# Two more head pairs take VectorE's transposition of P, and a new order table

## The chip, the cores and the metric

The kernel runs on one core of a Trainium2 chip. The metric is device time in microseconds (us), from the first to the last instruction of one execution with what lies around it; lower is better. Five engines work side by side and wait for each other through semaphores: TensorE (PE in the rows, its weight loads PEld), VectorE (DVE), ScalarE (ACT), GpSimd (POOL) and SyncE (SP), which issues every transfer of this kernel.

## The reference

Causal attention over 4 batches of 12 heads, 448 tokens, head size 64, and then a gated MLP over the 768 joined features. Cut to what matters:

```python
scores = q @ k.T / sqrt(64), masked to the lower triangle
P = exp(scores - rowmax);  x = (P / rowsum(P)) @ v        # per batch and head
h = gelu(x @ w_in);  u, v = h[..., :512], h[..., 512:]
v_s = w_sg @ layernorm(v) * g_ln + b_sg                   # over the 448 tokens
out = x + (u * v_s) @ w_out
```

## The kernel before

Heads are taken two at a time: 24 pairs, 0 to 23, six to a batch. The steps of a pair are these. A load brings q and k (`qk`), another brings v (`vraw`). TensorE computes the scores in two groups into PSUM (L639, 8 matmul records a group). VectorE adds the mask and takes the row maximum (L653). ScalarE takes the exponential into P and sums its rows (L661). The sums are inverted, transposed and spread over the partitions through DRAM (`rd`, `rb`). P must then be transposed, since TensorE contracts over the partitions, and the transposed P, called `B`, is multiplied with v (L738, "PV"). VectorE scales the result (`xt`, L766), and it is stored (`xd`) and split into a high and a low part for the MLP.

The transposition of P has two forms, chosen by `flip = p >= FLIP`. With `FLIP = 8`, pairs 0 to 7 use TensorE: four groups of four 128x128 transpositions into PSUM (`tx`, `ty`, L708), each group moved to `B` by ScalarE (L715) or, for one group of each pair of batch 0, by VectorE (L713). Pairs 8 to 23 use VectorE, which transposes blocks of 32x32 (L696, two instructions a pair) into the array `A`, and four transfers of 256 KB, issued by SP (L700), carry it from `A` to `B`:

```python
for z in range(2):
    dve(PW, lambda z=z: nc.vector.transpose(A[ia]..., P[ib[z]]), Pk[z] + [kp], Ak, Tt, 1.105)
for i in (0, 2, 1, 3):
    dma(lambda i=i: nc.sync.dma_start(out=B_.t[:, 512 * i:512 * i + 512],
                                      in_=PP[ia][32 * i:32 * i + 32]...), Ak, [(B_, i)], Te, ...)
```

There is one `A` (`NA = 1`): it is the third of the three double P buffers, which pairs 2 and 5 also use as plain P. So a pair's transposition on VectorE waits until the transfers of the pair before have read `A`, and pair 6's would wait for TensorE's transpositions of pair 5. `B` has two buffers. PV takes the same 1,024 columns for each of the two heads in either form, in 20 matmul records a pair with the first form and in 32 with the second.

Between the pairs of a batch TensorE works on the MLP of the batch before, in groups of up to three matmuls (L796): v, u, s and o. The weights are loaded in parts, split by ScalarE, VectorE and GpSimd; w_out comes in 16 parts (`wout`, L564 to L574) while pairs 6 to 8 are under way.

The order of the work is written out in the table `ORDER`, which lists every step by its number (1,927 steps; 551 of them TensorE's, 245 SP's), in the order of planned starts. Each engine issues its own steps in that order, so an instruction that waits holds up everything behind it on its engine, and a transfer that waits on SP holds up every later transfer. Eight PSUM banks are shared by all of it.

Of the kernel before, what the change touches and what calls it, by code (L numbers as in the profile page):

```python
# [50 lines left out]
FLIP = 8  # L51
# [367 lines left out]
def attention_gated_mlp(ctx: ExitStack, tc: tile.TileContext, qk, vP, w_in, g_ln, w_sgT, b_sg, w_out, out):  # L419
# [200 lines left out]
    def pair(p):  # L620
# [3 lines left out]
        per = STEP[b]  # L624
        flip = p >= FLIP
        kp, ks = "P" if p % (NP // 2) else "P0", "sm" if p % NS else "sm0"
# [379 lines left out]
```

## Time and profile before

| | us |
|---|---|
| median of 3 runs | 354.4 (353.96 to 354.82) |
| the profiled execution, its own time | 355.62 |
| its span, first to last instruction | 353.8 |
| what lies around the span | 1.8 |
| TensorE busy / VectorE / ScalarE / GpSimd | 339.1 / 260.0 / 196.6 / 149.9 |

A busy time is the union of an engine's instructions in the span; the rest of the span it was idle. Busy is not the same as needed: a matmul whose end is late counts as busy too.

### The profile page before, as it was taken

How to read it: one execution, taken by the hardware profiler on the slowest of the kernel's cores; microseconds unless marked ns; L12 is line 12 of the kernel's file. 1: busy time of each engine (PE TensorE's matmuls, PEld its weight loads, DVE VectorE, ACT ScalarE, POOL GpSimd, SP SyncE). 2: the span in 40 equal slices, each digit the busy share in tenths (PEclk: the TensorE clock that was granted, in tenths of full speed). 3: DMA queues.
4: the chain of work that ended last, by engine and by line, in shares of the span. 5: the costliest groups of instructions: out<-in, count | busy, mean ns of one | idle time of the engine just before them, and what ended most of it. 6: DMA issues, size and time to landing. Idle time of an engine off the chain costs nothing.

```text
span 353.8 us, 6879 instructions
## 1 busy us (share of the span) xinstructions
PE 339.1 (96%) x2231; PEld 269.2 (76%) x2231; DVE 260.0 (73%) x762; ACT 196.6 (56%) x658; POOL 149.9 (42%) x200
## 2 busy tenths in 40 slices
PE   7698999989999999999999999998999999999995
PEld 3455667657888778776898888776898898889995
DVE  2999978689999988756899987377897721258613
ACT  2999987777856957237443885218344700135410
POOL 4567887236977720010653641001265700242550
PEclk9999999999999999999999999999999999999999
DMA  7988987697855887797575786889465455400004
GB/s 237 374 284 292 304 287 228 196 287 210 248 123 173 219 238 250 242 298 248 151 173 128 235 236 176 269 240 295 121 200 126 139 119 196 155 2 1 0 2 156
DMA packets 37972, 69.50 MB, mean 196 GB/s; under 512 B 3888, under 2 KB 18992, under 8 KB 37936
## 3 DMA queue, kind: packets, MB, share of 16 engines
q1 hardware_dynamic: 37936, 69.06, 64.2%
q8 instruction: 18, 0.29, 0.3%
q14 instruction: 18, 0.15, 0.1%
HBM read 39.68 MB, written 12.58 MB: 148 GB/s over the span
## 4 chain that ended last, share of the span: by engine, by line
PE 69%; DMA 13%; DVE 9%; ACT 4%; SPq 3%; issue 1%; POOL 1%; DVEq 0%; POOLq 0%
PE m L796 47%; PE o L738 10%; PE s L639 8%; DMA B<-P 5%; ACT P L661 3%; DVE s L653 3%; DVE P L696 2%; DMA vn<-in_w_in_dram 2%; DMA out_dram<-res 2%; DMA rb<-rd 2%; PE tx L708 1%; DMA g<-in_w_out_dram 1%; DMA res<-xd 1%; PE ty L708 1%; SPq L680 1%
## 5 line engine op out<-in xcount | busy, mean ns | idle before, releaser
L661 ACT ACTIVATE P<-s,ngm 64x64 f32<-64x64 f32 (+3 forms) x240 | 100.3, 432 | 38.6 <-DVE ngm L653 18.4
L653 DVE CUSTOM_DVE_ANT_0 s<-s,mask 128x192 f32<-128x192 f32 (+3 forms) x192 | 75.3, 444 | 5.8 <-PE s L639 5.8
L796 PE MATMUL m<-win,x 128*128 128x512 f32 (+1 forms) x264 | 67.1, 399 | 0.0
L796 PE MATMUL m<-x,win 128*128 128x448 f32 x288 | 64.1, 370 | 1.8 <-ACT P L661 1.1
L796 PE MATMUL m<-g,wout 128*128 128x448 f32 x288 | 62.1, 368 | 0.0
L796 PEld LDWEIGHTS m<-x,win 128*128 128x128 f32 x288 | 53.3, 188 | 8.4 <-ACT P L661 1.9
L796 PEld LDWEIGHTS m<-g,wout 128*128 128x128 f32 x288 | 53.4, 188 | 5.4 <-issue 0.2
L796 PEld LDWEIGHTS m<-win,x 128*128 128x128 f32 (+1 forms) x264 | 46.8, 183 | 12.5 <-ACT P L661 0.6
L639 PE MATMUL s<-qk 64*128 64x448 f32 (+3 forms) x384 | 53.5, 403 | 1.8 <-DMA qk<-in_qk_dram 1.7
L639 PEld LDWEIGHTS s<-qk 64*128 64x128 f32 (+1 forms) x384 | 33.6, 178 | 23.2 <-issue 13.2
L661 ACT ACTIVATION_READ_ACCUMULATOR P<-s,ngm 128x1 f32 (+1 forms) x240 | 49.6, 207 | 0.0
L738 PE MATMUL o<-B,vraw 128*64 128x64 f32 (+4 forms) x672 | 47.2, 292 | 2.0 <-ACT P L661 1.4
L777 POOL TENSOR_TENSOR x<-xt,x 128x448 fp32r<-128x448 f32 x24 | 27.8, 1162 | 46.1 <-ACT x L776 45.9
L696 DVE STREAM_TRANSPOSE P<-P 128x1024 f32<-128x1024 f32 x32 | 39.3, 1233 | 9.5 <-DMA B<-P 4.4
L738 PEld LDWEIGHTS o<-B,vraw 128*64 128x64 f32 x672 | 33.0, 137 | 15.9 <-issue 6.3
L796 PE MATMUL m<-wsg,vn 128*128 128x448 f32 x176 | 39.6, 369 | 0.0
L851 POOL TENSOR_TENSOR mv<-mv,mhalf 128x1 f32<-128x1 f32 (+1 forms) x16 | 9.4, 592 | 67.7 <-DVE mv L849 67.2
L796 PEld LDWEIGHTS m<-wsg,vn 128*128 128x128 f32 x176 | 32.7, 188 | 3.2 <-issue 0.2
L804 ACT ACTIVATE tmp<-m 128x448 f32<-128x448 f32 (+1 forms) x28 | 15.2, 565 | 22.7 <-PE m L796 21.1
L807 ACT ACTIVATE tmp<-tmp 128x448 f32<-128x448 f32 (+2 forms) x32 | 18.9, 603 | 14.4 <-DVE tmp L805 14.1
L653 DVE DVE_READ_ACCUMULATOR2_ANT ngm<- 128x1 f32 (+1 forms) x192 | 25.7, 134 | 0.0
L805 DVE SCALAR_TENSOR_TENSOR tmp<-tmp,m 128x448 f32<-128x448 f32 (+1 forms) x28 | 17.3, 633 | 11.2 <-ACT tmp L804 11.1
(77 smaller groups left out, 379.5 us busy)
## 6 DMA issues: line engine op xcount, KB each, us to landing
B<-P SPq DMA_DIRECT2D x64, 256.0 KB
qk<-in_qk_dram SPq DMA_DIRECT2D x24, 448.0 KB
vn<-in_w_in_dram SPq DMA_DIRECT2D x12, 512.0 KB
vraw<-in_vP_dram SPq DMA_DIRECT2D x24, 256.0 KB
rb<-rd SPq DMA_DIRECT2D x24, 256.0 KB
xd<-xt SPq DMA_DIRECT2D x24, 224.0 KB
res<-xd SPq DMA_DIRECT2D x9, 448.0 KB
out_dram<-res SPq DMA_DIRECT2D x9, 448.0 KB
```

The source lines that it names most:

```text
L639: nc.tensor.matmul(out=s[z][bk].t[0:w, col:col + n], lhsT=qk_.t.rearrange("p a s -> p (a s)")[r, q0:q0 + w], rhs=qk_.t[r, 1, 0:n], start=T ...
L653: nc.vector.tensor_tensor_reduce(out=o, in0=o, in1=mk, scale=-0.125, scalar=3e38, op0=ALU.add, op1=ALU.min, accum_out=ngm[ib[z]][c][0:m])
L661: act(n, lambda c=c, m=m, k0=k0, n=n, bk=bk, col=col, off=off, kc=kc, i=i, z=z: nc.scalar.activation(out=P[i][0:m, off:off + n], in_=s[z][ ...
L696: dve(PW, lambda z=z: nc.vector.transpose(A[ia][:, :, :, z, :].rearrange("p g t k -> p t g k"), P[ib[z]]), Pk[z] + [kp], Ak, Tt, 1.105)
L708: nc.tensor.transpose(out, P[ib[z]][:, col:col + 128], ident)
L738: nc.tensor.matmul(out=dst(o.t[r]), lhsT=vr.t[:, c, r], rhs=src(z), start=first and n == 0, stop=last and n == len(lst) - 1)
L777: pool_tt(S, lambda: nc.gpsimd.tensor_tensor(out=y.t[:, S + 64:], in0=x.t, in1=f(y.t)[:, 0:S], op=ALU.subtract), [x, y], [(y, 1)], Ty)
L796: nc.tensor.matmul(out=ps.t[0:l().shape[1], 0:n], lhsT=l(), rhs=rr(), start=(k == 0), stop=(k == len(mms) - 1))
L804: act(n, lambda: nc.scalar.activation(out=z(), in_=h(), func=AF.Square), [ps], [t], at)
L805: dve(n, lambda: nc.vector.scalar_tensor_tensor(out=z(), in0=z(), scalar=1.0 / GC, in1=h(), op0=ALU.add, op1=ALU.mult), [ps], [t], at)
L807: act(n, lambda: nc.scalar.activation(out=z(), in_=z(), func=AF.Tanh, scale=GS * GC), [], [t], at, True)
L851: od.add("pool", 0.46, lambda mv=mv, m=m: nc.gpsimd.tensor_tensor(out=mv.t[0:m, 1:2], in0=mv.t[0:m, 1:2], in1=mhalf[0:m], op=ALU.pow), ["s ...
```

## The change

`FLIP` goes from 8 to 6: pairs 6 and 7, the first two of batch 1, take the second form of the transposition, and their v is laid out for it on the host. `ORDER` is replaced as a whole; it now has 1,923 steps (543 of TensorE, 409 instead of 417 of ScalarE, 542 instead of 538 of VectorE, 253 instead of 245 of SP). No other line differs. The diff, with the table cut:

```diff
-FLIP = 8
+FLIP = 6
...
 ORDER = (
-    1, 2, 84, 12, 4, 3, 118, 18, 5, 128, 6, 0, 172, 7, 24, 8, 162, 9, 10, 348, 85, 13, 14, 86, 15, 87, 16, 89, 11,
...
-    1921, 1897, 1922, 1898, 1902, 1925, 1923, 1890, 1926, 1924, 1903, 1891, 1904, 1892, 1905,
...
+    1921, 1919, 1910, 1922, 1920, 1911, 1912, 1886, 1913, 1897, 1887, 1914, 1891, 1888, 1892, 1904, 1893, 1905,
+    1894, 1898, 1906, 1899, 1907, 1900, 1901,
 )
```

Read by steps, SP's part of the table around pairs 6 and 7 was `p5 rb, p4 xd, p10 qk, p6 rd, p7 v, p6 rb, p5 xd, p7 rd, wout x4, p11 qk, wout x4, p7 rb, wout x3, p8 v, p6 xd, wout x2, p8 B x3`. It becomes `p5 rb, p4 xd, p10 qk, p6 B x4, p6 rd, p5 xd, p7 v, wout x5, p7 rd, p6 rb, wout x3, p11 qk, p7 rb, wout x2, p7 B x4, wout x2, p12 qk, wout x3, p6 xd, p8 v, p8 rd, p8 B x3`.

## Rows read from the trace of the kernel before

**Rows 1.** The page: busy time and share by engine; granted TensorE clock in 40 slices.
```profile
PE 339.1 (96%) x2231; PEld 269.2 (76%) x2231; DVE 260.0 (73%) x762; ACT 196.6 (56%) x658; POOL 149.9 (42%) x200
...
PEclk9999999999999999999999999999999999999999
```

**Rows 2.** Stretches: us, busy of PE, PEld, DVE, ACT, POOL; clock, DMA share, GB/s.
```profile
0.00:10.00 10.00, 6.40 (x23) 2.76 (x23) 3.80 (x20) 3.13 (x5) 5.45 (x28) 1.00 0.79 257
10.00:40.00 30.00, 25.74 (x188) 15.96 (x190) 29.18 (x105) 29.46 (x114) 20.97 (x22) 1.00 0.92 316
...
50.00:80.00 30.00, 28.61 (x212) 19.95 (x212) 22.24 (x82) 22.96 (x85) 14.20 (x22) 1.00 0.75 239
...
80.00:120.00 40.00, 40.00 (x276) 32.82 (x275) 39.77 (x122) 29.06 (x91) 30.38 (x45) 1.00 0.68 190
160.00:250.00 90.00, 88.06 (x586) 71.73 (x584) 71.13 (x190) 49.69 (x176) 25.66 (x29) 1.00 0.73 208
...
350.00:354.00 4.00, 0.29 (x2) 0.00 (x0) 0.96 (x2) 0.00 (x0) 0.00 (x0) 0.79 0.43 152
```

**Rows 3.** Groups of instructions: TensorE's and VectorE's transpositions, ScalarE's moves, the multiplication with v.
```profile
L708 PE MATMUL ty<-ident,P 128*128 128x128 f32 x64 | 10.4, 279 | 0.7 <-ACT B L715 0.4 <-ACT P L661 0.2
...
L715 ACT ACTIVATE B<-tx 128x512 f32<-128x512 f32 x16 | 9.7, 609 | 1.5 <-PE tx L708 1.4
...
L696 DVE STREAM_TRANSPOSE P<-P 128x1024 f32<-128x1024 f32 x32 | 39.3, 1233 | 9.5 <-DMA B<-P 4.4 <-ACT P L661 3.2 <-DMA vraw<-in_vP_dram 1.9
```

**Rows 4.** The chain that ended last, TensorE's pieces: start us, us, what.
```profile
37.53 1.89 PE o L738 x20
...
45.01 1.06 PE s L639 x8
46.08 0.59 PE tx L708 x4
46.66 0.44 PE ty L708 x4
...
102.98 0.61 PE m L796 x3
...
113.70 2.85 PE s L639 x24
116.56 4.68 PE m L796 x22
...
123.17 1.92 PE o L738 x32
```

**Rows 5.** The same chain where it leaves TensorE.
```profile
71.02 5.10 DMA g<-in_w_out_dram
76.14 0.38 ACT g L566
76.52 1.15 ACT P L661 x6
77.72 1.96 PE o L738 x20
...
156.16 7.00 DMA B<-P
163.29 1.25 DVE P L696
...
231.83 4.74 DMA B<-P
```

**Rows 6.** The page's transfers: queue with packets, MB, share of 16 engines; issues.
```profile
q1 hardware_dynamic: 37936, 69.06, 64.2%
...
B<-P SPq DMA_DIRECT2D x64, 256.0 KB
```

**Rows 7.** SP's timeline from 55 to 85 us: start, us, issues.
```profile
68.41 3.04 SPq L564 DMA_DIRECT2D g<-in_w_out_dram  x4
...
83.36 2.58 SPq L700 DMA_DIRECT2D B<-P  x3
```

188 rows, old and new, of the table ORDER are left out of this document.

## Prediction

> **What bounds the kernel now.** I read the busy times first, then the stretches, then the chain of work that ended last, and then the transfers. TensorE is busy for 339.1 of 353.8 us and its granted clock is full in every slice [rows 1], so what is left to gain is either TensorE work or TensorE's 14.7 us of idle time. The stretches say where that idle time lies: 7.9 us in the first 40 us (10 less 6.40, 30 less 25.74), 1.4 us between 50 and 80, 1.9 us between 160 and 250, 3.5 us after the last matmul; nothing elsewhere [rows 2]. In the first part VectorE and ScalarE are full (29.2 and 29.5 of 30 us), so there TensorE follows them. From 80 to 120 VectorE is full again, 39.8 of 40, but TensorE is too [rows 2]. The chain runs along TensorE and leaves it in two ways that matter here: a late w_out part holds ScalarE, which then holds pair 6's PV, and late transfers into B hold VectorE's next transposition [rows 5].
>
> **What the change removes.** Pairs 6 and 7 each lose four groups of four transpositions. A record lasts 279 ns [rows 3], but they overlap: a group that follows work of the same tile shape ends 0.44 us after it [rows 4]. Eight groups by 0.44 are 3.5 us off TensorE, which has no idle time around them but the 1.4 us above. ScalarE loses eight moves of 0.609 us [rows 3], 4.9 us; worth nothing by itself, since at 50 to 80 ScalarE has 7 us idle already [rows 2].
>
> By the Trainium skill ("VectorE: DVE Perf Modes", "The three transpose paths") a 128x128 transposition takes TensorE 390 ns (bf16); 32 of them would be 12.5 us, and the time some 343. The row decides for 0.11 us each, as the groups' ends are 0.44 us apart.
>
> **What it adds on TensorE.** PV of a pair goes from 20 records in 1.89 us to 32 in 1.92 [rows 4]: 0.06 us for both. The new table costs more: counted along TensorE's steps, the tile shape (scores, PV, all others) changes 87 times instead of 81. A change costs 0.15 us before a transposition (0.59 against 0.44), 0.17 before scores (1.06 for one group; 2.85 for three, so 0.9 for each further one) and 0.2 before MLP matmuls (22 in 4.68 us, where 3 without a change take 0.61) [rows 4]. Six more are 0.9 to 1.3 us; I take 1.2, near the upper price, since the changes into MLP groups are among the six. TensorE's work falls by 3.5 - 0.06 - 1.2 = 2.2 us.
>
> **What it adds elsewhere.** VectorE gets four transpositions of 1.233 us [rows 3], 4.9 us. The table puts pair 6's just before pair 8's scores and pair 7's around pair 9's; by the TensorE work in front of them that is about 60 to 78 us in the old trace. Between 50 and 80 VectorE has 7.8 us idle [rows 2], so I cost them at nothing there; without that cover they cost up to 4.9 us. Eight transfers of 256 KB are 2.1 MB; at 64.2% of 353.8 us for 69.06 MB [rows 6] they take 6.9 us of all 16 engines, where 25% of 30 us, 7.5 us, are free [rows 2]. On SP they take 0.86 us each (three in 2.58) [rows 7], 6.9 us too. Behind pair 6's four on SP stand its sums (`rd`), pair 5's store, pair 7's v, and the first w_out parts; behind pair 7's four stand w_out parts, pair 12's q and k, and pair 8's v. Who waits for those is ScalarE and VectorE, which split w_out in order with the exponentials and row maxima behind. Pair 6's PV stands about 16 us of TensorE work behind its last transfer in the table, pair 7's about 17; a landing takes 4.7 to 7.0 us from its issue [rows 5]. So the transfers themselves hide.
>
> **The idle time under the new table.** Four parts.
> The first 40 us: the table moves steps, but takes no work from VectorE or ScalarE there, and the same steps come up to pair 5's scores. I take no change, bounds -1 to +1.
> The 1.4 us before pair 6's PV: ScalarE stood 5.1 us behind a w_out part [rows 5]. In the new table, each w_out part has 3.9 us or more of TensorE work between issue and first use instead of 3.3, and pair 6's PV comes after more of u. I take half of the stall away, 0.7; bounds -1.4 to +1.4 (as long a stall again).
> 160 to 250 us: with one A, the next pair's transposition waits for the last transfer of the pair before. Between these two the old table puts at least 5.9 us of TensorE work; the new one puts 4.8, 4.9, 5.1 and 5.2 in four places (pairs 12, 21, 18 and 11), and is otherwise alike (median 6.9 against 6.8): late landings may have been in the search's objective, but these margins did not grow. Were every landing at the slow end, 7.0, the sum of what is short would be 5.3 us in the old table and 10.0 in the new. VectorE did wait 4.4 us for B in the old trace [rows 3], and TensorE's idle time there was 1.9, 0.44 of that. So the new table's 4.7 us more would be 2.1 us of TensorE; at the fast end, 4.7, nothing. I take 0.7, bounds -1.9 (all of that idle time goes) to +2.1.
> The end: the last groups and the last store are the same steps, no change.
> The parts cancel: -0.7 and +0.7.
>
> **Sum.** The profiled execution's 355.62 us becomes 353.4; its span 351.6. It stands 1.2 us above the median of the runs, 354.4, so for the median the forecast is 354.4 - 2.2 = **352.2 us**.
>
> **The rivals.** (1) The gain is eaten by late landings: the four short places and the later w_out parts cost TensorE 1.5 to 2.9 us more than now. For it: those margins lie at the fast end of what landings took. Against it: TensorE has MLP work in hand there (88.1 of 90 us busy [rows 2]). Time 353.7 to 355.1.
> (2) VectorE becomes the bound from pair 6 on, and the kernel gets slower. The place is the stretch up to 120 us: if pair 7's two transpositions (5 us of TensorE work apart in the table) slip past 80, they fall where VectorE has 0.2 us free in 40 [rows 2], and every later row maximum and GELU step of batch 1 slips with them. The price is up to 4.9 us; from 2.9 us on it outweighs the gain and shows as slower. Time 355.2 to 357.1. For it: idle time of 7.8 us for 4.9 us of work leaves only 2.9, and steps in order can't use all of it. Against it: pair 8's transpositions move back by some 10 us of TensorE work to make room, and pair 8 was early before (its PV stood 17 us behind its transfers).
> The Trainium skill's rule on the same page ("Rules for kernel authors") is to give a full 128x128 transposition to TensorE where PSUM will do, which is what this change leaves; it points to this rival.
> (3) The table is worth more than the transpositions: the stalls at pair 6 and at 160 to 250 both go, and a little of the start: -1.4, -1.9 and -0.5 on top of 2.2. Time 348.4 to 350.
>
> **How the numbers follow.** Forecast, 350 to 353.7 us: 0.58. Rival 1, 353.7 to 355.1: 0.17. Rival 2: 0.13. Rival 3: 0.12. Faster by over 0.2% (0.7 us, about what a measurement of this kernel can tell from no change) are the forecast and rival 3: 0.70; within: 0.17; slower: 0.13. The range leaves out the better half of rival 3 and the worse part of rival 2: 349.3 to 355.6. The likeliest case's own range is 350.6 to 353.7.
>
> **What would show each step.** TensorE's transposition rows at L708 fall from 128 to 96 and its busy time to about 337; L715 from 26 to 18; L696 rises from 32 to 36 and B's transfers from 64 to 72. VectorE between 50 and 80 fills to 27 us or more; between 80 and 120 TensorE stays full. The wait of pair 6's PV on ScalarE is gone or short. VectorE's wait for B rises from 4.4 us to 5 to 9. What would make the forecast wrong: idle time of TensorE between 50 and 125 us (rival 2), VectorE's wait for B over 9 us with TensorE idle behind it (rival 1), or TensorE's idle time below 13 us in all (rival 3).

## The result, and the profile after

The changed kernel takes 350.06 us (median of 4 runs, 348.92 to 351.6), against 354.42 (353.96 to 354.82) for the kernel before on the same chip: a ratio of 0.988, interval 0.984 to 0.992. The forecast was 352.2 with a range of 349.3 to 355.6. Its profiled execution took 350.24 us with a span of 348.4.

The stretches after, columns as in [rows 2]:

```profile
10.00:40.00 30.00, 26.52 (x184) 16.63 (x186) 27.98 (x113) 29.87 (x119) 20.85 (x22) 1.00 0.94 326
50.00:80.00 30.00, 30.00 (x185) 20.72 (x185) 26.91 (x95) 22.05 (x83) 14.68 (x23) 1.00 0.82 258
80.00:120.00 40.00, 38.96 (x290) 31.00 (x288) 38.03 (x103) 24.90 (x75) 30.78 (x44) 1.00 0.76 216
160.00:250.00 90.00, 89.80 (x657) 73.19 (x657) 73.31 (x211) 54.13 (x190) 28.44 (x32) 1.00 0.75 217
```

TensorE is full from 50 to 80, where VectorE now does 26.9 us of work instead of 22.2, and nearly full from 160 to 250. It lost 1.0 us between 80 and 120, where it had lost none. Two lines of the page as in [rows 1, 6], and two groups as in [rows 3]:

```profile
PE 335.8 (96%) x2223; PEld 266.6 (77%) x2223; DVE 260.3 (75%) x766; ACT 192.9 (55%) x650; POOL 148.8 (43%) x200
...
B<-P SPq DMA_DIRECT2D x72, 256.0 KB
```
```profile
L708 PE MATMUL tx<-ident,P 128*128 128x128 f32 x48 | 7.8, 282 | 0.5 <-ACT P L661 0.4
...
L696 DVE STREAM_TRANSPOSE P<-P 128x1024 f32<-128x1024 f32 x36 | 43.9, 1226 | 4.2 <-DMA B<-P 3.4 <-ACT P L661 0.6
```

VectorE's wait for B is 3.4 us, where it was 4.4 [rows 3] and the prediction said 5 to 9. The chain that ended last (start us, us, what), from 76 to 112 us, shows what TensorE waits for in the new place:

```profile
76.61 6.48 DMA g<-in_w_out_dram
...
84.09 0.70 DVE tmp L809
84.84 1.67 PE s L639 x7
...
110.66 0.60 DVE tmp L908
111.31 1.13 PE s L639 x4
```

A busy share hides small waits, so I also followed TensorE step by step. For each step of the table I took the time from the end of the step before to its own end. For each kind of step, with and without a change of the tile shape, the median of these times in the kernel before counts as its work, in every run alike; what is over is called idle time. It is a little below nothing where steps were shorter than that median, and it includes steps that ran long at a lower clock (last section). Work and idle time add up to the end of the last matmul less that of the first. The columns with two numbers are the idle time in that part of the span, by the end of the step. Each line is one execution. All times in us:

| profiled execution | work | idle, all | 0-41 | 41-80 | 80-125 | 125-160 | 160-255 |
|---|---|---|---|---|---|---|---|
| before | 331.08 | 16.48 | 10.03 | 1.77 | 0.12 | 0.20 | 4.32 |
| after | 328.84 | 13.28 | 9.12 | 0.46 | 3.31 | -0.04 | 0.36 |
| flip_only | 327.58 | 26.69 | 9.41 | 5.91 | 7.57 | 0.04 | 3.71 |
| table_only | 332.98 | 15.61 | 9.15 | 4.58 | 1.81 | 0.02 | 0.00 |
| new_then_old | 328.98 | 20.53 | 9.56 | 0.41 | 5.39 | 1.41 | 3.72 |
| old_then_new | 331.19 | 11.63 | 10.06 | 0.10 | 1.13 | -0.13 | 0.39 |
| flip_room | 327.58 | 31.11 | 9.32 | 10.41 | 6.60 | 0.31 | 3.14 |
| flip_room_then_new | 327.69 | 23.46 | 9.86 | 9.63 | 3.54 | -0.11 | 0.48 |
| new_late | 331.14 | 19.14 | 9.82 | 0.68 | 0.32 | 0.17 | 8.11 |
| q_loads_later | 331.08 | 12.02 | 9.99 | 0.25 | 1.05 | 0.18 | 0.45 |
| q23_later | 331.08 | 13.23 | 9.52 | 0.05 | 0.48 | 0.15 | 3.03 |
| q_early_tiny | 331.08 | 12.60 | 9.32 | 0.74 | 0.39 | 0.08 | 2.16 |
| after_less_vector | 328.84 | 12.49 | 8.83 | 0.43 | 3.09 | -0.14 | 0.21 |
| after_q_later | 328.84 | 11.49 | 9.76 | 0.43 | 1.30 | -0.08 | 0.01 |

The first two lines are the result in short. TensorE's work fell by 2.24 us, as forecast. The late idle time fell by 4.0 where I had it rise by 0.7, and 3.2 us of new idle time stand at 80 to 125 where I had none. Work and idle time together fell by 5.4 us, the medians of the runs by 4.4, as the profiled execution of the kernel before took 1.2 us more than its median. The runs below ask where each of these two comes from.

### The profile page after: what moved, and what is told of

It reads as the page before. It is cut to its first block, busy times and chain, and to the rows that moved or that the text cites. A ratio compares the mean times of both kernels' runs of the same rounds, so it can differ in the third digit from the quotient of the medians.

```text
span 348.4 us, 6885 instructions
## 1 busy us (share of the span) xinstructions
PE 335.8 (96%) x2223; PEld 266.6 (77%) x2223; DVE 260.3 (75%) x766; ACT 192.9 (55%) x650; POOL 148.8 (43%) x200
## 4 chain that ended last, share of the span: by engine, by line
PE 80%; DVE 10%; DMA 5%; POOL 2%; ACT 1%; issue 1%; SPq 0%; DVEq 0%; POOLq 0%; ACTq 0%
PE m L796 56%; PE o L738 11%; PE s L639 10%; DVE s L653 3%; DMA vn<-in_w_in_dram 3%; DMA g<-in_w_out_dram 2%; PE tx L708 1%; DVE ngm L653 1%; PE ty L708 1%; POOL win L574 1%; DVE vn L570 1%; ACT P L661 1%; DVE P L696 1%; DVE tmp L805 1%; PE s L675 1%
## 5 line engine op out<-in xcount | busy, mean ns | idle before, releaser
L661 ACT ACTIVATE P<-s,ngm 128x448 f32<-128x448 f32 (+3 forms) x240 | 100.4, 433 | 36.1 <-DVE ngm L653 32.1
L796 PE MATMUL m<-win,x 128*128 128x512 f32 (+1 forms) x264 | 66.3, 397 | 0.0
L639 PE MATMUL s<-qk 64*66 64x64 f32 (+3 forms) x384 | 54.0, 399 | 3.3 <-DMA qk<-in_qk_dram 2.2
L696 DVE STREAM_TRANSPOSE P<-P 128x1024 f32<-128x1024 f32 x36 | 43.9, 1226 | 4.2 <-DMA B<-P 3.4
L738 PEld LDWEIGHTS o<-B,vraw 128*64 128x64 f32 x696 | 34.1, 137 | 14.3 <-issue 7.0
L776 ACT ACTIVATE x<-xt 128x448 fp32r<-128x448 f32 x18 | 10.4, 577 | 43.0 <-DVE xt L766 39.8
L912 POOL TENSOR_TENSOR tmp<-tmp,g 128x448 f32<-128x448 f32 x16 | 18.2, 1148 | 20.5 <-DVE tmp L908 14.0
L805 DVE SCALAR_TENSOR_TENSOR tmp<-tmp,m 128x448 f32<-128x448 f32 (+1 forms) x28 | 17.6, 639 | 12.4 <-ACT tmp L804 12.4
```

The source lines that it names most:

```text
L639: nc.tensor.matmul(out=s[z][bk].t[0:w, col:col + n], lhsT=qk_.t.rearrange("p a s -> p (a s)")[r, q0:q0 + w], rhs=qk_.t[r, 1, 0:n], start=T ...
L661: act(n, lambda c=c, m=m, k0=k0, n=n, bk=bk, col=col, off=off, kc=kc, i=i, z=z: nc.scalar.activation(out=P[i][0:m, off:off + n], in_=s[z][ ...
L696: dve(PW, lambda z=z: nc.vector.transpose(A[ia][:, :, :, z, :].rearrange("p g t k -> p t g k"), P[ib[z]]), Pk[z] + [kp], Ak, Tt, 1.105)
L738: nc.tensor.matmul(out=dst(o.t[r]), lhsT=vr.t[:, c, r], rhs=src(z), start=first and n == 0, stop=last and n == len(lst) - 1)
L776: act(S, lambda: nc.scalar.activation(out=y.t[:, 0:S], in_=x.t, func=AF.Copy), [x], [y], Ty, True)
L796: nc.tensor.matmul(out=ps.t[0:l().shape[1], 0:n], lhsT=l(), rhs=rr(), start=(k == 0), stop=(k == len(mms) - 1))
```

## The experiments

Two orders can be cut and joined: `OLD` is the table of before, `NEW` that of the changed kernel, with steps of the same meaning carried over to the other's numbers. A kernel takes its time beside the kernel before on the same chip (medians 354.14, 354.24 and 354.68 in the three sets). Four questions follow one another.

**Is it the transposition or the table?** Four kernels separate them.

flip_only:

```diff
-FLIP = 8
+FLIP = 6
# OLD without the TensorE transpositions of pairs 6 and 7; SP's part of it:
 p6 rd
+p6 B x4
 p7 v
...
 wout
+p7 B x2
 p7 rb
+p7 B x2
 wout
```

> The old table with FLIP = 6: only pairs 6 and 7's transpositions and moves are replaced, by VectorE's two and the four transfers, set in at the places of the old ones. Shape changes on TensorE stay 81. Theory A (the two parts of the change add up: 3.5 us less of TensorE work from the transpositions, the rest from the later part of the table): TensorE work down 3.4 us, the idle time at 160 to 250 us stays at about 2 us visible, time 350.5 to 351.8. Rival B (the transpositions are only worth something with the room that the new table makes on VectorE before 80 us): 353.5 or more, with TensorE idle between 60 and 110 us.

Measured: 362.03 us, ratio 1.020 (1.014 to 1.027): the transposition alone, in the old order, costs 8 us. The work fell by 3.5 us as counted, but TensorE waited 2.97 us for pair 7's sums (the step that transposes them, L675, at 66.2 us) and 5.42 for pair 8's. The chain behind the second:

```profile
74.14 1.11 DVE P L696
...
75.30 0.55 SPq L700
...
78.11 1.04 SPq L700
79.20 5.58 DMA B<-P
84.90 1.25 DVE P L696
...
89.31 0.21 DVE rs L672
89.66 0.37 PE s L675
```

Pair 7's transfers stand behind eight loads of w_out in SP's queue, but SP had issued all eight: the first transfer went out at 75.30, right behind the transposition (74.14 plus 1.11). So what came late was pair 7's transposition on VectorE. The landing of its transfers holds pair 8's transposition, and that holds VectorE's whole queue with the sums that TensorE needs.

table_only:

```diff
 FLIP = 8
-ORDER = OLD
+ORDER = NEW, with the TensorE transpositions of pairs 6 and 7 put where their VectorE ones stood
```

> The new table with FLIP = 8: pairs 6 and 7 keep TensorE's transpositions, set in where the new table has VectorE's. 92 shape changes on TensorE. Theory A: 3.5 us more of TensorE work than the changed kernel and about 0.8 for five more shape changes, so 353.5 to 355, no faster than before. Rival C (the table alone makes the gain, TensorE's removed work having been hidden): 350 to 351.5.

Measured: 356.98 us, 1.0074 (1.004 to 1.011), above both expectations. The late idle time is gone, 0.00, but the first part costs 4.58 us of idle time at 41 to 80 and 11 more shape changes (92): without VectorE's transpositions the new first part is worse than the old one.

new_then_old, old_then_new:

```diff
-ORDER = NEW                                   # FLIP = 6
+ORDER = NEW[:780] + [n for n in OLD if n not in NEW[:780]]
-ORDER = OLD                                   # FLIP = 8
+ORDER = OLD[:784] + [n for n in NEW if n not in OLD[:784]]
```

> FLIP = 6; the new table up to about 113 us (its first 780 steps), then all other steps in the order of the old table. 89 shape changes. Theory A (the size that the prediction missed lies in the later part of the table): TensorE idle at 160 to 250 us comes back to 2 us visible, some 4 us with what its modelled ends hide; time 352.5 to 354. Rival D (late transfers got less late because of what changes before 113 us): late idle time stays away, 350 to 351.

> FLIP = 8; the old table up to about 113 us (its first 784 steps), then all other steps in the order of the new table. 81 shape changes, no transposition taken off TensorE. Theory A: the late idle time goes, 3 to 4 us, time 350.3 to 351.5. Rival D: 354 to 355, and the prediction's own step, the four shorter distances between a transfer's issue and the next transposition, would make it 354.5 to 356.

Measured: new_then_old 356.51 us, 1.006 (1.003 to 1.009); old_then_new 349.83, 0.985 (0.981 to 0.990). In new_then_old the late idle time came back, as theory A said (3.72 us), but the time is above both expectations: 5.39 us of idle time stand at 80 to 125 and 1.41 at 125 to 160, and nothing was run to explain those. So the later part of the table alone, with no transposition moved, makes a gain as large as the whole change: 349.83 beside 350.06. The two transpositions and the first part together come to nothing. After these four runs I held that the new order has other work ready for TensorE while VectorE waits; that is the rival of q_loads_later below, and it fell there. The price that I gave for VectorE's wait did not hold either: in old_then_new VectorE waits for B longer than before, 6.7 us in all against 4.4 [rows 3], and TensorE's late idle time is 0.39.

**Can the transposition's gain be had with more room?**

flip_room:

```diff
# flip_only with, in SP's queue:
-p6 rd, p6 B x4
+p6 B, p6 rd, p6 B x3
-wout x3, p11 qk, wout x4, p7 B x2, p7 rb, p7 B x2
+wout, p7 B, wout x2, p7 B, p11 qk, wout, p7 B, wout, p7 B, wout x2, p7 rb
# pair 7's transposition 2.4 us of TensorE work earlier, pair 8's later
```

> Kernel: the table of before everywhere, but pairs 6 and 7 are transposed by VectorE (FLIP 6), as in flip_only; other than there, the eight transfers of pairs 6 and 7 stand ahead of the w_out loads in SP's queue, pair 7's transposition comes 2.4 us of TensorE work earlier, and pair 8's transposition is moved a little later. 81 shape changes. Theory (the 7.9 us that flip_only lost are a matter of place: pair 7's transfers stood behind eight w_out loads and pair 8's transposition behind them): TensorE's idle time falls from 26.7 us to 16 to 18, the TensorE work stays at 327.6, and the time is 350.5 to 352.5. Rival (moving two pairs to VectorE and to transfers costs more than it saves in this stretch, wherever they are put): 357 us or more, with VectorE's wait for B near the 9.7 us of flip_only.

Measured: 365.23 us, 1.030 (1.024 to 1.035), worse than flip_only. The chain says why:

```profile
67.36 4.57 DMA B<-P
72.13 1.25 DVE P L696
...
75.46 0.55 SPq L700
76.05 0.59 SPq L564
...
81.51 1.43 SPq L700
82.98 5.85 DMA g<-in_w_out_dram
```

Pair 7's transposition waits for A until pair 6's transfers have landed and runs only at 72 to 75. Its four transfers stood between the w_out loads, not ahead of all of them as I had meant, and now stop those loads on SP. So VectorE, with pair 8's transposition behind, waits for a w_out part. The rival said "wherever they are put"; two placings don't show that, and the new first part holds 0.41 to 0.46 us of idle time at 41 to 80 with the same transpositions. I did not find which of its moves does that. And as SP had issued flip_only's w_out loads before the transposition ended, the turn behind them was not what flip_only had lost.

flip_room_then_new:

```diff
+ORDER = ROOM[:784] + [n for n in NEW if n not in ROOM[:784]]    # ROOM: flip_room's order
```

> Kernel: flip_room up to its 784th step (about 113 us), and from there the order of the changed kernel. Theory (the moved transpositions save 3.5 us of TensorE work, the later part of the table 4 us of idle time, and the two add up when the first has room): TensorE work 327.6 us, idle 12 to 13, time 346.5 to 348.5, below both kernels. Rival (the two draw on the same time of VectorE, and what one saves the other waits for, as in the changed kernel between 80 and 125 us): 349.5 to 351.

Measured: 359.07 us, 1.014 (1.010 to 1.018), above both expectations. The later part saves its 2.7 us again (3.14 to 0.48), the first part's loss stays.

**What does the later part of the table do?** Between 150 and 256 us the chain of the kernel before leaves TensorE for long stretches, and that of the changed kernel does not leave it once. The head of the chain in this window, with the shares by line: first before, then the changed kernel, then q_loads_later (below).

```profile
by line: PE m L796 28.4%; DMA B<-P 16.4%; PE o L738 8.8%; DVE P L696 7.9%; ACT P L661 5.8%; DMA out_dram<-res 5.5%; DMA rb<-rd 5.3%; DMA res<-xd 3.9%; PE s L639 3.2%; SPq L700 2.6%; DVE s L653 2.5%; SPq L680 2.4%; SPq L630 1.9%; issue 1.7%;
```
```profile
by line: PE m L796 67.6%; PE o L738 16.2%; PE s L639 15.3%; PE s L675 0.9%; issue 0.2%
```
```profile
by line: PE m L796 72.3%; PE o L738 14.3%; PE s L639 12.7%; PE s L675 0.8%; issue 0.2%
```

One piece of the old chain is a load of q and k (L630) that stands between pair 18's transfers (L700). It belongs to pair 23, whose scores come 56 us of TensorE work later. Before's chain from there to the wait of u on batch 2:

```profile
217.54 1.16 SPq L630
218.74 0.63 SPq L700
219.47 5.84 DMA out_dram<-res
225.38 4.17 DMA res<-xd
229.57 0.64 DVE res L939
...
241.10 2.57 ACT P L661 x11
...
244.78 2.18 PE m L796 x9
```

The load delays a store, SP waits for the store before it can issue the next load of `res` into the same buffer, VectorE waits for that load (L939), and the transfers behind come later: pair 19's last one (231.83 in [rows 5]), VectorE's next transposition, ScalarE's exponentials, and the PSUM bank that TensorE wants. The old table has four more such loads, of pairs 16 to 19, 22 to 57 us of TensorE work ahead of their scores. The new table has these four 9 to 20 us of TensorE work later, and pair 23's behind pair 18's transfers.

q_loads_later (SP's queue; no other engine's instructions change):

```diff
 p12 rd
-p16 qk
-p17 qk
 p11 rb
...
+p16 qk
 p14 rd
 o
-p18 qk
 p13 rb
...
 p12 xd
-p19 qk
 p15 rd
...
 p14 B
+p17 qk
+p18 qk
 p15 v
...
 p14 xd
+p19 qk
 p16 B
...
 p18 B
-p23 qk
 p18 B
...
 p19 B
+p23 qk
 p19 rb
```

> Kernel: before, with one edit to SP's queue alone: the q/k loads of pairs 16, 17, 18, 19 and 23, which stand 22 to 57 us ahead of their scores, are moved 9 to 36 us of TensorE work later (pair 23's behind pair 19's transfers instead of between pair 18's). Every other engine's instructions stay as they are. Theory (SP's backed-up queue and the load on the DMA engines make pairs 13 to 18's transfers late, VectorE's next transposition waits for them, and ScalarE and TensorE behind it): the 4.3 us of TensorE idle time at 160 to 255 us fall to 1.5 to 2.5, the time to 351.5 to 353. Rival (the idle time hangs on the order of TensorE's own work, which has nothing ready at these places): 353.8 to 354.5 us, late idle time 4 or more.

Measured: 350.4 us (median of 10 runs), 0.989 (0.987 to 0.992). Five loads moved in one queue give what the whole new table gives; the late idle time is 0.45 us, below what even this theory expected. TensorE's order was the same as before, so the rival falls. That the new table gains in the same way is argued from the places of the loads in its queue and not shown: no run puts the early loads back into it. And the lead alone is not what costs. Counted along TensorE's steps, the changed kernel issues q and k of pairs 20, 22 and 23 some 28, 34 and 53 us ahead of their scores, and its late idle time is 0.36 us; none of them stands between a pair's four transfers, as pair 23's does in the old table. 160 to 250 of q_loads_later:

```profile
160.00:250.00 90.00, 89.80 (x651) 73.75 (x650) 73.02 (x194) 51.03 (x177) 26.06 (x30) 1.00 0.75 215
```

new_late:

```diff
+ORDER = OLD[:1214] + [n for n in NEW if n not in OLD[:1214]]    # joined at 179 us of TensorE work
```

> Kernel: the order of before up to its 1214th step (about 179 us of TensorE work), then the order of the new table, with pairs 6 and 7 on TensorE as before. 81 shape changes. Theory (each stall is mended where it stands: of before's 4.3 us after 160, about 3.2 lie behind 190): idle at 160 to 255 falls to 1.1 to 1.5 and the time to 350.8 to 351.6. Rival (the new order gets its slack between 113 and 179 us, by running TensorE's and SP's work in an order that leaves them a lead, and its last part alone gives little): 353 to 354.5 us.

Measured: 359.42 us, 1.015 (1.010 to 1.020): slower than before, which neither side expected. 5.44 of its 8.11 us of late idle time are one wait, for pair 17's sums at 198 us, behind a pile of VectorE's steps at the joint. It says that a joint of two tables is not neutral, and nothing on its question.

q23_later:

```diff
 p18 B
-p23 qk
 p18 B
...
 p19 B
+p23 qk
 p19 rb
```

> Kernel: before, with one q/k load moved, pair 23's, from between pair 18's four transfers to behind pair 19's (11.6 us of TensorE work later; its scores come 44 us after that). Theory (each early load delays the transfers right behind it and no others): of before's 4.3 us of late idle time the 2.1 us behind 230 go and the 2 us between 165 and 200 stay; 351.8 to 352.8 us. Rival (the loads of pairs 16 to 19 push the whole chain late, and this one adds nothing): 353.8 to 354.5 us.

Measured: 352.44 us, 0.994 (0.991 to 0.996), inside the expected 351.8 to 352.8. No idle time over 0.15 us is left behind 200 us; what stays are 1.82 us at 164, 0.53 at 190 to 192 and 0.74 at 196, 3.1 in all. So the early load of pair 23 delays what stands behind it in its own part, and by q_loads_later the other four own the waits before 200 us. (The wait near 164 us differs between executions, 0.2 to 1.8 us with the old later part.) The chain of this run shows the one at 164 still there:

```profile
152.43 1.35 SPq L700
...
154.59 7.39 DMA B<-P
162.11 1.25 DVE P L696
...
163.98 8.39 PE m L796 x39
```

q_early_tiny:

```diff
# q_loads_later, and at the five old places, on SP:
+nc.sync.dma_start(out=scr[p], in_=qk[p][:, 0, 0:8])
```

> Kernel: q_loads_later, and at each of the five places that its q/k loads left in SP's queue a load of 4 KB (128 rows of 32 bytes) into a tile of its own that nothing reads. So the queue has as many entries at the old places as in before (five more in all), and the bytes of the q/k loads travel late. Theory of the queue (what the early loads cost is their turn in SP's queue, 0.4 to 1.2 us each ahead of the next transfers): the gain of q_loads_later goes again, 353 to 354.5 us, late idle time 3 or more. Rival, the theory of the bytes (448 KB each on DMA engines that are 80% busy there hold up the transfers behind them): 349.8 to 351 us, late idle time below 1.

Measured: 352.27 us (median of 8 runs), 0.995 (0.992 to 0.997), late idle time 2.16 us. It lies between the two expectations, and the intervals of this and of q_loads_later don't meet. Of q_loads_later's 1.1%, about 0.6 go again when only the turns in the queue come back (0.9949 - 0.9891), and some 0.5 stay with the bytes: in sum both count, about alike. By place they do not. With the turns alone back, the idle time at 180 to 205 us is 1.68 us (1.12 before, 0.49 in q_loads_later), but that behind 225 us is 0.24 where before has 2.16: there it was the bytes of pair 23's load, and not its turn, in this one execution. A load of 4 KB holds SP as long as one of 448 KB in the same place (all five together 4.6 us against 4.0). First SP's timeline of this run, where the small load (L963) stands between pair 18's transfers, then that of before, the load itself:

```profile
214.69 0.55 SPq L700 DMA_DIRECT2D B<-P  x1
215.28 1.16 SPq L963 DMA_DIRECT2D scr<-in_qk_dram  x1
216.49 0.76 SPq L700 DMA_DIRECT2D B<-P  x1
```
```profile
217.54 1.16 SPq L630 DMA_DIRECT2D qk<-in_qk_dram  x1
```

The Trainium skill ("DMA: Bandwidth & Descriptors", "Rules for kernel authors") says to issue a DMA early and to wait on its semaphore late. These runs show the other side of it: with one queue for all transfers, five loads 22 to 57 us early cost 4 us, and 11 to 21 us (44 for pair 23) were early enough.

**What is the new idle time at 80 to 125?** VectorE is 38.0 of 40 us busy there, and one of the waits begins with a late w_out load.

after_less_vector:

```diff
-nc.vector.scalar_tensor_tensor(out=lo(), in0=hi(), scalar=3, in1=lo(), ...)
+nc.vector.scalar_tensor_tensor(out=lo()[:, 0:w], in0=hi()[:, 0:w], scalar=3, in1=lo()[:, 0:w], ...)   # w = 8 for w_out
```

> Kernel: the changed kernel, but VectorE's second operation on each piece of w_out (the one that joins the two words, 24 times 0.4 to 0.5 us) covers 8 of 192 columns, so w_out is not rebuilt and the output is not the reference's. Every step keeps its place. It takes some 8 us of work from VectorE, about 4 of them between 80 and 112 us. Theory (VectorE, 9.9 of 10 us busy from 90 to 120, is what TensorE waits for in the 3.3 us of idle time at 80 to 125): idle time there falls to 1.2 or less, time 347.3 to 348.6. Rival (TensorE waits there for late w_out transfers and for the order of steps): 349.5 to 350.6 us.

Measured: 348.97 us, 0.984 (0.981 to 0.986), between the two expectations; idle time at 80 to 125 3.09 us instead of 3.31. But the edit took less than I said: there are 16 such operations and not 24, and one on 8 columns still lasted 293 ns in the mean instead of 486, and VectorE was busy for 37.09 us of 80 to 120 instead of 38.03. So it speaks against VectorE's bound only weakly.

after_q_later (SP's queue of the changed kernel):

```diff
 wout
-p11 qk
 p7 rb
...
 wout
-p12 qk
 wout
...
 wout
+p11 qk
 p9 v
...
 p9 B
-p13 qk
 p9 rb
+p12 qk
 p8 xd
...
 p9 xd
+p13 qk
 p14 qk
-p15 qk
 p10 rb
...
 p12 rb
+p15 qk
 p12 B
```

> Kernel: the changed kernel with one edit to SP's queue alone: the q/k loads of pairs 11, 12 and 15 are moved 21, 22 and 16 us of TensorE work later and that of pair 13 12.6 later, out of the stretch in which the w_out loads come in (TensorE's first wait in 80 to 125 us ends with a w_out load that took 6.5 us to land, at 76.6 to 83.1). They still stand 11 to 20 us ahead of their scores. Theory (what q_loads_later showed holds here too: early loads take from transfers that are waited for): idle time at 80 to 125 us falls from 3.3 to 1.5 to 2.4, time 348.2 to 349.4, below both kernels. Rival (VectorE bounds that stretch, so loads change nothing): 349.7 to 350.6 us, idle time there 3 or more.

Measured: 349.79 us (median of 6 runs, 348.36 to 351.4), 0.986 (0.984 to 0.989). In the profiled execution, the fastest of the six, the idle time at 80 to 125 fell to 1.30, a little below what was expected, and the span is 346.6 instead of 348.4. The median misses the expected 349.4 and can't be told from the changed kernel's: its six runs spread over 3 us, at granted clocks of 0.994 to 1.000. So the mechanism shows in the trace and a gain in time is not established. The stretch:

```profile
80.00:120.00 40.00, 39.60 (x301) 31.93 (x301) 39.55 (x114) 25.53 (x78) 32.50 (x47) 1.00 0.80 217
```

VectorE is fuller than in the changed kernel (39.55 against 38.03) and TensorE waits less. As far as one execution of each tells, two of the three us were thus not VectorE's load but transfers that came late beside early q and k loads. Pair 7's four transfers are not what made the w_out load at 76.61 late on their own: SP issues them right behind it in both kernels, and the wait of 0.96 us that began with that load is gone here. The rest, 0.49 at 102.9 and 0.64 at 110.0, still follows VectorE's queue.

## Why the prediction was right, and where it was not

The time came out 2.1 us better than forecast and inside the range. Two errors above all went against each other, the late idle time (4.7 us better than forecast) and the one at 80 to 125 (3.2 us worse); that the sum fell inside the range is in good part luck.

- *TensorE's work, -2.2.* Right: -2.24. Eight groups at 0.44 us, six more shape changes. L708 fell to 96 records (48 each for `tx` and `ty`), L715 to 18. The page's busy time fell to 335.8 where I said about 337.
- *VectorE's 4.9 us hidden between 50 and 80.* Right: 26.91 us busy there, TensorE full.
- *The transfers hidden.* Right: 72 transfers, DMA share 0.82 instead of 0.75 from 50 to 80, 0.46 us of idle time from 41 to 80. Behind 80 they are one of several streams beside which a w_out load came late.
- *The first 40 us, no change within 1.* -0.9 by step, within the bounds; the nine runs with the old first part give 9.3 to 10.1 and the five with the new one 8.8 to 9.8, so one execution can't tell a difference from the spread.
- *Pair 6's stall, -0.7.* It went wholly, 1.57 to nothing at 70 to 80. But five of the runs that keep the old first part and pairs 6 and 7 on TensorE have only -0.1 to 0.6 there, and 0.3 to 1.1 at 80 to 125 where before has 0.1. I costed one execution's wait as if it belonged to the order; it is about what that execution took above its median.
- *160 to 250, +0.7.* This is the step that failed: -4.0. I counted the TensorE work between a pair's last transfer and the next transposition, found it shorter in the new table, and priced a longer wait of VectorE at 0.44 of TensorE's time. VectorE's wait did not say what TensorE lost: in old_then_new it rose to 6.7 us at 0.39 us of idle time; and in the changed kernel it fell to 3.4 us, so the late landings that I counted did not come. What TensorE waited for before was the row of late work behind five early q and k loads, as q_loads_later shows; the new table issues four of these later and the fifth behind pair 18's transfers. I had listed only the loads around pairs 6 and 7 when I went through SP's queue. I also saw 1.9 us of idle time there in [rows 2], where the count by steps has 4.3: a busy TensorE row includes matmuls that run on a late operand.
- *80 to 120 stays full.* Wrong: 3.3 us of idle time. Rival 2 named the place and VectorE as the cause. The place is right; after_q_later puts some 2 of the 3.3 on late transfers, about 1.1 still follow VectorE's queue.
- *Rival 3* (the table worth more than the transpositions) is what happened in kind: stalls at pair 6 and at 160 to 250 both went. Its time, 348.4 to 350, was missed by the idle time at 80 to 125; without those 3.2 us the changed kernel would take some 346.9, an estimate from the table. Rival 1, late landings, did not occur. Two of the prediction's own signs of being wrong came, rival 2's idle time between 50 and 125 us and rival 3's less than 13 us in all (12.6, the span of 348.4 less 335.8), and they offset each other in the time.

That the two transpositions and the new first part together save work and then give it back is shown by old_then_new: without them the work is 2.35 us more and the idle time from 41 to 125 is 2.5 us less, and the time is the same. Not settled: which moves of the new first part make room for pairs 6 and 7 on VectorE, whether the new later part gains by the places of its loads alone, and whether any order would keep those 2.35 us whole.

## What to carry to other kernels

A load that is issued far ahead is not free when one queue carries all transfers: it takes a turn and bandwidth from the transfers behind it. Give it the lead that it needs, and look at what stands right behind it before giving it more. Before pricing a wait by the instruction that waits, follow the chain back from the engine that sets the end; here a VectorE wait of 4.4 us stood beside 4.3 us of late idle time, and one of 6.7 us beside 0.4. When a whole table changes, run its halves alone: here the half that the change's description left out was enough for the gain.

## What the runs showed of the hardware

Four more VectorE transpositions, 4.6 us, raised VectorE's busy time by 0.3 us only [rows 1], since other operations got shorter: the 64x512 forms of L853 and L805 from 1258 to 530 and from 1344 to 709 ns in the mean, four of each, while the 128x512 form of L853 rose from 622 to 704. In the kernel before, one L853 of 64x512 lasted 2.47 us beside two operations of GpSimd, while one of 128x512 at 87.02, with GpSimd idle, lasted 0.53. VectorE's timeline, and GpSimd's:

```profile
87.02 0.53 DVE L853 TENSOR_SCALAR tmp<-tmp,mv 128x512 f32<-128x512 f32 x1
...
183.64 2.47 DVE L853 TENSOR_SCALAR tmp<-tmp,mv 64x512 f32<-64x512 f32 x1
```
```profile
183.57 2.25 POOL L777 TENSOR_TENSOR x<-xt,x 128x448 fp32r<-128x448 f32 x2
```

By the Trainium skill ("SBUF — State Buffer", "Who interferes with whom") VectorE and GpSimd share a pair of ports; where a VectorE instruction uses that pair, as a tensor_scalar can, whichever of the two issues first holds it for its whole instruction. The rows agree: GpSimd's work starts at 183.57, VectorE's at 183.64, and VectorE's ends at 186.11, behind both of GpSimd's at 185.82. Between these two executions of L853 lie 1.9 us.

TensorE's granted clock also made a wait cost more than its own length. In flip_room TensorE waited 3.5 us at 67 us for pair 7's sums, and the clock granted from 65 to 75 was 0.66, so about two thirds of the time at the lower of its levels (1.2 of 2.4 GHz); before has 1.00 there. These are 5 us stretches of flip_room:

```profile
65.00:70.00 5.00, 2.86 (x13) 1.54 (x15) 1.22 (x4) 1.51 (x8) 1.96 (x3) 0.66 0.72 164
70.00:75.00 5.00, 4.81 (x22) 3.01 (x18) 2.87 (x8) 0.61 (x2) 0.00 (x0) 0.66 0.84 258
```

From 70 to 75 TensorE counts as busy for 4.81 us with 22 matmuls, where before has 5.00 with 25. The three groups of scores that follow the wait each took 0.85 to 0.94 us longer than their median. In flip_only the steps right behind its two long waits took 3.9 us more than their medians in all, at granted clocks of 0.75 and 0.90 (65 to 70 and 70 to 75 us) and 0.52 (90 to 95); the table counts this as idle time.
